# A new kernel of small units: attention by head pairs, the first V turned on TensorE, and a range test of the softmax sums on GpSimd

## The chip, the cores and the metric

The kernel runs on one core of a Trainium2 chip. The metric is the device time of one execution in microseconds (us). TensorE multiplies (PE in the profile, its weight loads PEld), VectorE (DVE) and ScalarE (ACT) evict PSUM and do the pointwise work, GpSimd (POOL) issues the input loads and a few pointwise steps, SyncE (SP) issues the other transfers.

## The reference, cut to what matters

B, H, S, D are 4, 8, 768, 64; a sequence has 8 blocks of 96.

```python
P = sort_net                                   # [B, H, 8, 8]
for _ in range(5):                             # Sinkhorn
    P = exp(P - max(P, -1))
    P = P / (sum(P, -1) + 1e-9)
    P = P / (sum(P, -2) + 1e-9)
k_sorted = einsum('bhij,bhjcd->bhicd', P, k_blocks)   # blocks of K and V mixed by P
v_sorted = einsum('bhij,bhjcd->bhicd', P, v_blocks)
attn = softmax(q_blocks @ k_sorted.T / 8)             # inside each block of 96
x = (attn @ v_sorted) as [B, S, 512]
wq, wk = x @ w_q, x @ w_k                             # 64 wide
mixed = ((wq @ wk.T) / 8) @ x
out = relu(mixed) @ w_out                             # [4, 768, 512] float32
```

Both kernels compute `mixed` as `wq @ (wk.T @ x)`, and neither subtracts the row maximum before the softmax's exponential.

## The kernel before, in words

The kernel has one block of straight code. Work is cut into units, each a small function `u_<letter>(b, n, ...)` with b the batch and n the part, and a string `ORDER` names every unit in the order in which it is recorded. Each engine executes its own instructions in that order and waits on semaphores for the others, so `ORDER` fixes what stands ahead of what on every engine. A capital letter is TensorE work (its last digit is the first PSUM bank), the small letter behind it the eviction of that bank, by ACT (`A`) or DVE (`D`).

The units of one batch, in the order of the data:

- `l`: the loads of Q, K, V on GpSimd's queue, 768 KB each (three buffers of each); `N`: a one-element copy on GpSimd that makes it wait for a certain tile, so that the next load is not issued earlier.
- `c` (lines 150 to 163): the five Sinkhorn rounds, DVE with ACT's exponential, once for all batches. `U`, `b`, `B`: the small matrix is turned on TensorE, copied, and spread over the 128 partitions by eight matmuls with the pattern `Lx`. `n`: M, the block mixing matrix of four heads in the form that TensorE takes, by DVE for batch 0 and by GpSimd for the others, which read `PTR`, an SBUF copy made by `u`.
- `Q`/`q`: Q turned by identity matmuls, a third of the rows of all heads in one unit; `K`/`k`: K sorted and turned in one step, one pair of heads in one unit, out of two banks; `V`/`v`: V sorted, a third of the rows of all heads, evicted to `Vs`.
- `R`: six transfers on SP's queue, 130 KB each, that move the sorted V of a batch from `Vs` into `VT`, where the 96 rows of a block lie on the partitions. All six must have landed before the first `P` of the batch.
- `S`/`e`: scores and exponential for five (block, head pair) items in one unit, seven units a batch; `P`: attention times V, 14 heads' blocks in one unit, five a batch; `r`, `x`: the reciprocals of the sums (column 64 of each product) and the scaled product, DVE.
- `T`/`t`, `J`/`j`, `W`/`w`, `G`/`g`, `H`/`h`, `O`/`o`: the token MLP: X turned, wq and wk, wk turned, wk.T @ x, mixed with relu, output. `d`: half of `qkT` moved by SP to other partitions. `y`: output transfers on SP, a third of a batch each, 512 KB.
- `Z`: matmuls on a zeroed tile `fil` whose result nobody reads, 64 in all; eight at the start, the others between the units of batches 0 and 1.

In S and P of the kernel before an item's number runs over blocks first and head pairs inside a block, so the first group of products needs all four head pairs of K and Q.

Of the kernel before, what the change touches and what calls it, by code (L numbers as in the profile page):

```python
# [14 lines left out]

ORDER = """
l00P l01P l02P i00P i03P i02P l11P c00D Z087 c01D i01D c02D Z027 c03D Z127 c04D Q026 Q007 q02D c05D
Q015 Z224 q01A q00D U006 Z423 b00D Z322 B003 n00D u00A Z522 n11P n01D Z622 K010 K032 n10P k01A K024  # L20
k03D Z727 k02A N02k l03P Z1026 V000 V022 v00A K004 v02D V016 k00A N00k l12P l10P Z821 R01S n21P v01D
R00S K112 S000 R04S S044 n20P e00A k11D S066 e06A R02S K100 e04A S012 R05S S036 R03S k10A Z1125 Z924
e03A K120 K134 e01A k12D S026 e02A k13D P002 S050 r00D Z1227 e05A x00D N00x l21P P014 V106 r01D P030
x01D v10A P042 r04D P024 r03D x04D T007 x03D V112 t00A R10S v11A r02D Q106 x02D R11S Q127 T031 q12A
Q110 q10D T015 t03D q11A N11q l20P l31P l04P l32P l30P T024 V122 t01A S100 n31P v12D S156 t02A J005
e10A n30P S122 R12S j00D J014 R15S e15A K200 R14S j01D W005 R13S e12A w00D W014 S116 w01D G005 e11A
K232 G015 k23A K216 g01D k20A k21D S144 P112 e14A P100 r11D K226 x11D P134 k22A r10D Q213 r13D x10D
S166 Q202 q21A x13D T101 q20A Q220 t10D S134 e16A q22D e13A K322 P146 k32D S250 S214 e25A r14D P122
x14D e21A K330 r12D S246 d00S x12D k33A K304 e24A k30D S220 T123 T112 e22A t12D K314 S236 t11D T133
k31A S260 J102 t13D e23A S204 d01S j10D J113 e26A N26e l22P e20A V306 V310 v30D j11A W102 H024 v31A  # L30
W113 w11D V326 w10D h02D G103 v32A H000 d10S R30S Q312 h00D Q325 q31A G113 q32D Q304 g11A H010 O057
q30D h01A S312 o05D S324 e31A S330 O036 R34S e32A R35S V222 o03D R33S O007 e33A v22D R32S d11S V214
R31S V200 o00D v21A R25S S342 O016 R24S v20D e34A R23S H114 R22S O027 o01D R20S R21S H100 P322 o02A
h11D y00S O046 h10A r32D S304 x32D y01S o04A O107 e30A P240 y02S P232 o10A r24D P214 x24D P226 r23D
r21D O131 x23D O120 r22D o13A x21D T233 o12A P201 x22D t23A S364 y11S O110 e36A r20D T223 x20D o11A
T217 P304 t22A y10S T202 r30D t21A H120 x30D J213 t20A P316 j21D h12A S354 J202 r31D d21S x31D e35A
W213 O141 j20D T300 w21D o14A d20S P334 t30D W207 P342 r33D O156 w20D x33D G207 o15A r34D T311 x34D
T320 y12S t31A G217 t32D T336 g21A J301 t33D H222 H214 j30D J310 h22A d30S W301 H206 j31A w30D O243
h20A d31S W312 G301 o24D h21A O250 w31D O227 o25A G311 y22S o22A O230 g31A H302 H324 o23A O211 h32A
y21S H316 O200 o21D O351 h30D h31A O345 o20A o35D O314 y20S o34D O307 o31A y32S O325 o30A O334 y30S  # L40
o32A o33A y31S
# [4 lines left out]
def kernel(  # L46
# [35 lines left out]
    sb = ctx.enter_context(tc.tile_pool(name="sb", bufs=1))  # L82
# [6 lines left out]
    ENG = {"A": nc.scalar, "D": nc.vector, "P": nc.gpsimd, "S": nc.sync}  # L89
# [8 lines left out]

    def load(t, src, b):
        nc.gpsimd.dma_start(out=t[b % NIN].rearrange("p h r d -> p h (r d)"),  # L100
                            in_=src[b].rearrange("h (p r) d -> p h (r d)", p=P))

    QT = tiles("QT", 2, [P, NP, R6, P])
    KT = tiles("KT", 2, [P, NP, S + P - BLK])
    Vs = tiles("Vs", 2, [P, R6, H, D1])
    VT = tiles("VT", 2, [BLK, NB, H * D1])
    E = tiles("E", 2, [BLK, NT, EW])
    X = tiles("X", 2, [BLK, NB, DM])
    XT = tiles("XT", 2, [P, PT, NB, BLK])
# [4 lines left out]
    mixT = tiles("mixT", 1, [P, 2, 2, R6, P])  # L114
# [3 lines left out]
    R = tiles("R", 4, [BLK, 2, 7], FP32)  # L118
    PTR = sb.tile([P, NB, BH], BF16, name="PTR")
    Pb = sb.tile([BH, NB, NB], BF16, name="Pb")  # L120
    PbT = sb.tile([NB * NB, BH], BF16, name="PbT")
    Lx = sb.tile([NB * NB, NB, NB, SP], BF16, name="Lx")
# [3 lines left out]
    gate = sb.tile([1, 1], BF16, name="gate")  # L126
# [21 lines left out]


    def u_c(b, n, e):  # L150
        if n == 0:
            nc.vector.memset(Pm[:, NB:NB + 1, :], 1e-9)
            nc.vector.memset(fil, 0.0)  # L153
# [3 lines left out]
        nc.scalar.activation(Pv, Pv, ACT.Exp)  # L157
# [3 lines left out]
        nc.vector.reduce_sum(tmp, Pm.rearrange("p i j -> p j i"), axis=AX.X)  # L161
        nc.vector.reciprocal(tmp, tmp)
        nc.vector.tensor_mul(Pb if n == 5 else Pv, Pv, cols(tmp))


    def u_i(b, n, e):
        if n == 0:
            nc.gpsimd.memset(idb, 0.0)
            nc.gpsimd.affine_select(out=idb, in_=idb, compare_op=ALU.not_equal, fill=1.0, base=0,
                                    pattern=[[-1, P]], channel_multiplier=1)  # L170
        elif n == 1:
            nc.vector.reduce_max(m_p, idb.rearrange("p (j s) -> p s j", s=SP), axis=AX.X)
        elif n == 3:
            nc.gpsimd.memset(Lx, 0.0)
            nc.gpsimd.affine_select(out=Lx.rearrange("p i j s -> p (i j) s"),
                                    in_=Lx.rearrange("p i j s -> p (i j) s"),
                                    compare_op=ALU.not_equal, fill=1.0, base=0,
                                    pattern=[[-1, NB * NB], [0, SP]], channel_multiplier=1)
        elif n == 2:
            for t in Vs:  # L180
                nc.gpsimd.memset(t[:, :, :, D:D1], 1.0)
            for t in KT:
                nc.gpsimd.memset(t[:, :, S:S + P - BLK], 0.0)
            for t in E:
                nc.gpsimd.memset(t[:, :, 2 * TH * BLK:EW], 0.0)
                nc.gpsimd.memset(t[:, NT - 1, 2 * (NB * NP - TH * (NT - 1)) * BLK:EW], 0.0)


    def u_l(b, n, e):
        if n == 3:  # L190
            for s, w in enumerate((moe_w_q, moe_w_k)):
                nc.gpsimd.dma_start(out=wqk[:, :, s, :], in_=w.rearrange("(t p) d -> p t d", p=P))
        elif n == 4:
            nc.gpsimd.dma_start(out=wo, in_=moe_w_out.rearrange("(t p) d -> p t d", p=P))
        else:
            load((Qn, Kn, Vn)[n], (q, k, v)[n], b)


    def u_U(b, n, bank):
        mm(bf(bank)[0:NB * NB, 0:BH], Pb.rearrange("p i j -> p (i j)"), idb[0:BH, 0:BH], t=True)  # L200

    def u_b(b, n, e):
        nc.vector.tensor_copy(PbT, bf(U["t"])[0:NB * NB, 0:BH])

    def u_B(b, n, bank):
        for i in range(NB):
            mm(PS[:, bank, i * BH:(i + 1) * BH], Lx[:, i].rearrange("p j s -> p (j s)"), PbT)

    U = {}

    def u_n(b, n, e):
        h0, h1 = n * 4, n * 4 + 4
        if b == 0:
            src = PS[:, U["bank"], 0:NB * BH].rearrange("p (i h) -> p h i", h=BH)
        else:
            src = PTR.rearrange("p i h -> p h i")
        src = src[:, b * H + h0:b * H + h1, :]
        ENG[e].tensor_tensor(  # L218
            out=M[b % 2][:, h0:h1], in0=src.unsqueeze(2).to_broadcast([P, 4, SP, NB]),
            in1=m_p.unsqueeze(1).unsqueeze(3).to_broadcast([P, 4, SP, NB]), op=ALU.mult)  # L220

    def u_u(b, n, e):
        copy(e, PTR.rearrange("p i h -> p (i h)"), PS[:, U["bank"], 0:NB * BH])

# [6 lines left out]
    def u_Q(b, n, bank):  # L231
        ps = bf(bank).rearrange("p (k r s) -> p k r s", k=NP, r=2)
        for r in range(2):
            for kp in range(NP):
                for hh in range(2):
                    mm(ps[hh * D:(hh + 1) * D, kp, r, :], Qn[b % NIN][:, 2 * kp + hh, 2 * n + r, :],
                       idb, t=True)

    def u_q(b, n, e, bank):
        copy(e, QT[b % 2][:, :, 2 * n:2 * n + 2, :].rearrange("p k r s -> p k (r s)"),  # L240
             bf(bank).rearrange("p (k s) -> p k s", k=NP))


    def flat(bank, nb=2):
        return PS[:, bank:bank + nb, :].rearrange("p a n -> p (a n)")

    def u_K(b, n, bank):
        ps = flat(bank)
        for r in range(R6):
            for hh in range(2):  # L250
                h = 2 * n + hh
                mm(ps[hh * D:(hh + 1) * D, r * P:(r + 1) * P], Kn[b % NIN][:, h, r, :],
                   M[b % 2][:, h].rearrange("p s i -> p (s i)"))

    def u_k(b, n, e, bank):
        copy(e, KT[b % 2][:, n, 0:S].rearrange("p (i s r) -> p i s r", i=NB, s=SP),
             flat(bank)[:, 0:S].rearrange("p (r s i) -> p i s r", r=R6, s=SP))


# [6 lines left out]
    def u_v(b, n, e, bank):  # L266
        copy(e, Vs[b % 2][:, 2 * n:2 * n + 2, :, 0:D].rearrange("p r h d -> p h r d"),
             flat(bank).rearrange("p (h r d) -> p h r d", h=H, r=2))

    def u_R(b, n, e):  # L270
        ENG[e].dma_start(out=VT[b % 2].rearrange("(s r) i x -> r s i x", r=R6)[n],
# [198 lines left out]
```

## Time and profile before

| what | us |
|---|---|
| three runs | 125.07, 125.53, 125.67 |
| median | 125.53 |
| span of the profiled execution, first to last instruction | 123.3 |
| busy in it: PE, DVE, ACT, POOL | 101.9, 69.5, 69.2, 27.1 |
| first sorting matmul of K starts / last output matmul ends | 15.0 / 118.6 |

The page gives the profiled execution by its span; the median of the runs is 2.2 us above that span. Line 138 is the helper of all matmuls, lines 142 and 144 those of the copies by ACT and by DVE, so these groups are told apart by their tiles (`ps<-VT,E` is unit P). A matmul's listed duration is a latency of about 0.2 us and more, and successive ones overlap: what a unit costs TensorE is read from the length of a run of many against one of few. PEclk is the granted TensorE clock.

### The profile page before, as it was taken

The numbers are of one execution on the slowest core, as the hardware profiler recorded it, in microseconds if no ns is written. First come the engines' busy times: TensorE is split into PE (matmuls) and PEld (weight loads), VectorE is DVE, ScalarE is ACT, GpSimd is POOL, SyncE is SP. The second block draws the span as 40 slices with busy tenths as digits, with TensorE's granted clock in tenths as the row PEclk, the third lists the DMA queues.
The fourth block names the chain that finished last, engine by engine and source line by source line (L and its number), as shares of the span: only waits on it lengthen the run. The fifth ranks groups of instructions, "written<-read, shape, count | busy, mean of one in ns | idle before, by whom it ended". The sixth has DMA issues, their size and how long they took to land. (4 is left out here: it accounts for less than half of the span.)

```text
span 123.3 us, 3389 instructions
## 1 busy us (share of the span) xinstructions
PE 101.9 (83%) x1439; PEld 65.7 (53%) x1449; DVE 69.5 (56%) x132; ACT 69.2 (56%) x93; POOL 27.1 (22%) x42
## 2 busy tenths in 40 slices
PE   5818877692799999608998999999999999999940
PEld 2216464541447886508887677554767665443410
DVE  2879547305402976404769669497697885304500
ACT  4113155863301699900579977885669736855550
POOL 6993096910020029900000030000000000000000
PEclk9976999999679999995589999999999999999995
DMA  0999999899949426999999339947947104144493
GB/s 4 141 203 203 205 203 153 142 215 227 147 34 203 106 57 57 196 243 206 206 203 206 54 33 175 260 104 202 396 156 308 53 16 175 32 169 171 167 363 153
DMA packets 19950, 20.19 MB, mean 164 GB/s; under 512 B 2016, under 2 KB 18400, under 8 KB 19936
## 3 DMA queue, kind: packets, MB, share of 16 engines
q0 software_dynamic: 14064, 10.09, 56.9%
q1 hardware_dynamic: 5872, 9.89, 24.2%
q8 instruction: 11, 0.18, 0.6%
q14 instruction: 3, 0.02, 0.1%
HBM read 20.19 MB, written 6.29 MB: 215 GB/s over the span
## 5 line engine op out<-in xcount | busy, mean ns | idle before, releaser
L301 ACT ACTIVATE E<-ps 96x960 bf16<-96x960 f32 (+1 forms) x28 | 24.2, 906 | 7.7 <-PE ps L138 7.6
L138 PE MATMUL ps<-wo,mixT 128*128 128x512 bf16 x90 | 22.6, 380 | 0.6 <-issue 0.2
L333 DVE TENSOR_TENSOR X<-ps,R 96x896 bf16<-96x896 f32 (+1 forms) x20 | 19.7, 998 | 0.5
L138 PE MATMUL ps<-fil 128*128 128x512 bf16 x60 | 17.6, 438 | 2.0 <-DVE fil L153 1.2
L138 PE MATMUL ps<-VT,E 96*128 96x65 bf16 x256 | 11.7, 202 | 7.7 <-DMA VT<-Vs 7.2
L138 PEld LDWEIGHTS <-E 96*128 96x128 bf16 x256 | 10.3, 103 | 9.4 <-issue 8.5
L142 ACT COPY ot<-ps 128x512 f32<-128x512 f32 x16 | 9.4, 585 | 10.1 <-PE ps L138 9.2
L138 PEld LDWEIGHTS <-mixT 128*128 128x128 bf16 x96 | 8.2, 98 | 9.4 <-issue 1.3
L328 DVE RECIPROCAL R<-ps 96x14 f32<-96x14 f32 (+1 forms) x20 | 4.3, 222 | 15.4 <-PE ps L138 15.4
L138 PEld LDWEIGHTS <-fil 128*128 128x128 bf16 x64 | 6.5, 110 | 10.0 <-issue 4.4
L138 PE MATMUL ps<-idb,Qn 128*64 128x128 bf16 x192 | 9.2, 263 | 3.1 <-DMA Qn<-in_q_dram 3.1
L142 ACT CAST KT<-ps 128x768 bf16<-128x768 f32 x9 | 7.1, 800 | 6.8 <-PE ps L138 6.8
L142 ACT CAST Vs<-ps 128x1024 bf16<-128x1024 f32 x6 | 6.2, 1029 | 8.1 <-PE ps L138 7.8
L144 DVE CAST KT<-ps 128x768 bf16<-128x768 f32 x7 | 6.6, 956 | 6.7 <-PE ps L138 6.5
L138 PE MATMUL ps<-M,Kn 128*64 128x128 bf16 x192 | 8.3, 227 | 2.2 <-DMA Kn<-in_k_dram 0.9
L138 PEld LDWEIGHTS <-Qn 128*64 128x64 bf16 x192 | 7.7, 138 | 4.3 <-DMA Qn<-in_q_dram 3.6
L138 PE MATMUL ps<-QT,KT 64*128 64x96 bf16 x256 | 9.8, 207 | 0.2 <-ACT KT L142 0.2
L144 DVE COPY ot<-ps 128x512 f32<-128x512 f32 x8 | 5.5, 689 | 7.6 <-ACT ot L142 4.8
L406 ACT ACTIVATE mixT<-ps 128x1024 bf16<-128x1024 f32 x8 | 8.1, 1029 | 2.7 <-PE ps L138 2.6
L144 DVE CAST Vs<-ps 128x1024 bf16<-128x1024 f32 x6 | 7.2, 1222 | 3.0 <-PE ps L138 3.0
L138 PEld LDWEIGHTS <-Kn 128*64 128x64 bf16 x192 | 6.4, 113 | 4.5 <-issue 2.5
L218 POOL TENSOR_TENSOR M<-PTR,m_p 128x512 bf16<-128x512 bf16 x6 | 7.7, 1321 | 5.0 <-ACT PTR L142 4.9
(67 smaller groups left out, 132.9 us busy)
## 6 DMA issues: line engine op xcount, KB each, us to landing
out_dram<-ot SPq DMA_DIRECT2D x12, 512.0 KB, 2.8
VT<-Vs SPq DMA_DIRECT2D x24, 130.0 KB, 4.6
Qn<-in_q_dram POOLq DMA_DIRECT2D x4, 768.0 KB, 11.0
Kn<-in_k_dram POOLq DMA_DIRECT2D x4, 768.0 KB, 10.9
Vn<-in_v_dram POOLq DMA_DIRECT2D x4, 768.0 KB, 11.5
wo<-in_moe_w_out_dram POOLq DMA_DIRECT2D x1, 512.0 KB, 14.7
qD<-qkT SPq DMA_DIRECT2D x8, 48.0 KB, 2.3
wqk<-in_moe_w_q_dram POOLq DMA_DIRECT2D x1, 64.0 KB, 3.5
```

The source lines that it names most:

```text
L138: nc.tensor.matmul(o, w, x, is_transpose=t, start=start, stop=stop, skip_group_check=True)
L142: nc.scalar.copy(o, i)
L144: nc.vector.tensor_copy(o, i)
L218: ENG[e].tensor_tensor(out=M[b % 2][:, h0:h1], in0=src.unsqueeze(2).to_broadcast([P, 4, SP, NB]), in1=m_p.unsqueeze(1).unsqueeze(3).to_bro ...
L301: nc.scalar.activation(E[b % 2][:, n, 0:2 * w * BLK].rearrange("p (t a c) -> p a t c", a=2, c=BLK), PS[0:BLK, bank:bank + 2, 0:w * BLK].re ...
L328: nc.vector.reciprocal(rr[b, n][:, :, 0:w], avps(bank, w)[:, :, :, D])
L333: nc.vector.tensor_mul(xo.rearrange("p (a t d) -> p a t d", a=2, d=D), avps(bank, w)[:, :, :, 0:D], rr[b, n][:, :, 0:w].unsqueeze(3).to_br ...
L406: nc.scalar.activation(o, i, ACT.Relu)
```

## The change

- **Order.** `ORDER` is a new list with another order, other banks and other engines for the evictions. The `N` units are gone. Batch 0's loads are cut in halves (K's first half first); the loads of batch 1 follow without a wait.
- **Units by head pairs.** Q becomes four units of one head pair (768 columns) in place of three of 1024; S, P and X run over head pairs first and blocks inside, so the first scores need only the first pair. T turns one head pair (eight blocks) in one unit, and X, XT are laid out for that. H is three equal units of 256 columns, `mixT` has two buffers. W turns 128 rows in place of 64.
- **First V on TensorE.** For batch 0, V and its six transfers R are replaced by Y/y (sorted and turned as K is, into the other K tile) and F/f (turned back by 32 identity matmuls, and evicted straight into `VT`). Batches 1 to 3 keep V, v and R, with one `Vs` buffer in place of two.
- **Start.** `PbT` is made by DVE's transpose in place of U and b; `Lx` is made by an ACT copy from the identity and `m_p` by eight small matmuls and an ACT copy, in place of GpSimd's and DVE's steps; M of batch 0 is made by head pairs. The first `Z` unit has 28 matmuls and stands behind the matmuls for `m_p`; one other `Z` unit of two is left.
- **Range test and general path.** All reciprocals are kept in one tile `Rall` (96 partitions x 280). After everything that GpSimd does, `guard()` reduces it to its maximum and, negated in place, to its minimum, loads a flag into a register, and `tc.If` runs `general()` if a value lies outside 1e-20 to 1e20. `general()` computes the whole reference again with GpSimd alone. Its 14,528 instructions (with the waits among them) stand between GpSimd's part and the end; the other engines have none of it. With the inputs here it is jumped over.
- **End.** Batch 3's outputs leave in six transfers of 256 KB, the others as before.

```diff
 ORDER = """
-l00P l01P l02P i00P i03P i02P l11P c00D Z087 c01D i01D c02D Z027 c03D Z127 c04D Q026 Q007 q02D c05D
-...
+i02:D lk0a i00:G lq0a c00:D lq0b a01:A c01:D a02:A lk0b c02:D lv0a Z028:0 Q02:0 a03:A Q00:1 c03:D
+a04:A lv0b Q03:2 c04:D a05:A lp i03:G c05:D B00:3 n03:D:3 q03:A:2 Q01:4 n00:D:3 n02:D:3 q00:A:1 lq1
+K03:5 q01:D:4 lk1 u00:A:3 K02:1 k03:A:5 K00:4 n01:D:3 k02:D:1 q02:A:0 Y00:6 lv1 Y01:0 y00:D:6 K01:2
+Y03:6 k00:A:4 y01:A:0 S00:4 y03:A:6 n11:G F00:0 F03:1 f03:D:1 k01:A:2 Y02:6 n10:G y02:D:6 S05:2
+F01:1 e00:A:4 S01:4 F02:6 n21:G e05:A:2 e01:A:4 f02:D:6 S02:2 Q11:7 Q12:4 e02:A:2 f00:A:0 Q10:6
+...
+h11:A:6 O15:5 r32:D:0 P33:6 P31:2 W21:4 o15:A:5 O13:5 w21:A:4 r31:D:2 s02:S
+r33:D:6 O12:4 x33:D:6 x32:D:0 o13:A:5 s10:S P30:6 O14:5 W20:0 T32:1 x31:D:2 w20:A:0 d20:S T31:2
+t32:A:1 G20:3 r30:D:6 d21:S x30:D:6 G21:3 T30:6 g20:A:3 o14:D:5 t31:D:2 T33:7 H22:0 t30:D:6 o12:A:4
+...
+    def u_a(b, n, e, bank):
+        nc.scalar.activation(Pv, Pv, ACT.Exp)
+        if n == 2:
+            for j in range(NB):
+                mm(PS[:, 7, 0:SP], idb, idb[:, j * SP:(j + 1) * SP], start=(j == 0), stop=(j == NB - 1))
+            nc.scalar.copy(m_p, PS[:, 7, 0:SP])
+        elif n == 3:
+            nc.scalar.copy(Lx.rearrange("p a j s -> p (a j) s"),
+                           idb[0:BH, 0:BH].unsqueeze(2).to_broadcast([BH, BH, SP]))
...
+        if n == 5:
+            nc.vector.transpose(PbT, Pb.rearrange("p i j -> p (i j)"))
...
+    def u_Y(b, n, bank):
+        sort_turn(Vn, b, n, bank)
+    def u_y(b, n, e, bank):
+        in_blocks(KT[(b + 1) % 2], n, e, bank)
+    def u_F(b, n, bank):
+        for i in range(NB):
+            mm(bf(bank)[0:BLK, i * P:(i + 1) * P], KT[(b + 1) % 2][:, n, i * BLK:(i + 1) * BLK], idb, t=True)
+    def u_f(b, n, e, bank):
+        copy(e, VT[b % 2][:, :, 2 * n:2 * n + 2, 0:D],
+             bf(bank)[0:BLK, :].rearrange("p (i h d) -> p i h d", i=NB, h=2))
...
-            i, kp = divmod(pr, NP)
+            kp, i = divmod(pr, NB)
...
-        nc.vector.reciprocal(rr[b, n][:, :, 0:w], avps(bank, w)[:, :, :, D])
+        nc.vector.reciprocal(Rall[:, b, n, :, 0:w], avps(bank, w)[:, :, :, D])
...
+    def guard():
+        s1 = keep.tile([1, 2], FP32, name="s1")
+        flag = keep.tile([1, 1], mybir.dt.int32, name="flag")
+        g = nc.gpsimd
+        rv = Rall.rearrange("p b n a t -> p (b n a t)")
+        g.tensor_reduce(s1[:, 1:2], rv, axis=AX.XYZWC, op=ALU.max)
+        g.tensor_scalar(rv, rv, -1.0, None, op0=ALU.mult)
+        g.tensor_reduce(s1[:, 0:1], rv, axis=AX.XYZWC, op=ALU.max)
+        g.tensor_scalar(s1[:, 0:1], s1[:, 0:1], -1e-20, None, op0=ALU.is_le)
+        g.tensor_scalar(s1[:, 1:2], s1[:, 1:2], 1e20, None, op0=ALU.is_le)
+        g.tensor_tensor(s1[:, 0:1], s1[:, 0:1], s1[:, 1:2], op=ALU.mult)
+        g.tensor_scalar(flag, s1[:, 0:1], -1.0, 1.0, op0=ALU.mult, op1=ALU.add)
+        return g.value_load(flag[0:1, 0:1])
...
+    off = guard()
+    work.close()
+    with tc.If(off > 0):
+        with tc.tile_pool(name="gp", bufs=1) as gp, \
+                tc.tile_pool(name="gd", bufs=1, space=bass.MemoryType.DRAM) as dram:
+            general(nc.gpsimd, gp, dram)
```

More of the change, by code (lines that the diff above doesn't have):

```diff
@@ L24 @@
[L24 to L28, printed above, removed]
@@ new lines @@
+t12:D:4 e20:A:6 Q30:4 t13:D:3 S25:0 q32:D:5 H00:2 S26:6 q30:D:4 Q31:5 J10:4 e25:A:0 h00:D:2 e26:A:6
+lk3 S23:0 H02:6 S24:2 R21:S h02:D:6 j10:A:4 q31:D:5 O00:4 e23:A:0 K30:0 e24:A:2 R25:S k30:A:0 Q33:7
+R23:S R20:S o00:D:4 K32:2 k32:D:2 H01:5 P23:0 r23:D:0 x23:D:0 lv3 J11:4 h01:A:5 j11:A:4 P22:2 P20:5
+r22:D:2 x22:D:2 r20:D:5 O04:4 V30:0 P24:2 x20:D:5 d11:S r24:D:2 q33:A:7 o04:A:4 O01:7 v30:A:0
+o01:A:7 W11:4 K31:5 x24:D:2 K33:0 s00:S V31:2 w11:A:4 k33:D:0 T22:4 k31:A:5 d10:S T23:5 V32:6
+v31:A:2 P21:0 t23:A:5 W10:2 v32:A:6 t22:D:4 r21:D:0 O02:3 S32:4 R31:S w10:D:2 S36:6 G10:2 G11:2
@@ L170, in u_i @@
                                     pattern=[[-1, P]], channel_multiplier=1)
-        elif n == 1:
-            nc.vector.reduce_max(m_p, idb.rearrange("p (j s) -> p s j", s=SP), axis=AX.X)
-        elif n == 3:
[L174 to L183, printed above, removed]
+        elif n == 2:
+            nc.vector.memset(Pm[:, NB:NB + 1, :], 1e-9)
+            nc.vector.memset(fil, 0.0)
+            for t in KT:
+                nc.vector.memset(t[:, :, S:S + PAD], 0.0)
+        elif n == 3:
@@ L191, in u_l @@
+            nc.gpsimd.memset(Rall[:, :, NG - 1, :, (NU - AG * (NG - 1)) // 2:AG // 2], 1.0)
+    def u_l(b, n, e, bank):
+        if n == "p":
             for s, w in enumerate((moe_w_q, moe_w_k)):
                 nc.gpsimd.dma_start(out=wqk[:, :, s, :], in_=w.rearrange("(t p) d -> p t d", p=P))
-        elif n == 4:
+        elif n == "o":
             nc.gpsimd.dma_start(out=wo, in_=moe_w_out.rearrange("(t p) d -> p t d", p=P))
         else:
-            load((Qn, Kn, Vn)[n], (q, k, v)[n], b)
@@ L199, in u_U @@
[L199 to L203, printed above, removed]
+            t, src = {"q": (Qn, q), "k": (Kn, k), "v": (Vn, v)}[n[0]]
+            h0, h1 = {"": (0, H), "a": (0, H // 2), "b": (H // 2, H)}[n[2:]]
+            b = int(n[1])
+            nc.gpsimd.dma_start(out=t[b % NIN][:, h0:h1].rearrange("p h r d -> p h (r d)"),
+                                in_=src[b, h0:h1].rearrange("h (p r) d -> p h (r d)", p=P))
@@ L205, in u_B, with u_u @@
     def u_B(b, n, bank):
         for i in range(NB):
[L207 to L212, printed above, removed]
+            g, x = divmod(i, BH // NB)
+            mm(PS[:, bank, i * BH:(i + 1) * BH], Lx[:, x].rearrange("p j s -> p (j s)"),
+               PbT[:, g * BH:(g + 1) * BH])
+    def u_u(b, n, e, bank):
+        copy(e, PTR.rearrange("p i h -> p (i h)"), PS[:, bank, 0:NB * BH])
@@ L213, in u_n @@
+    def u_n(b, n, e, bank):
         if b == 0:
-            src = PS[:, U["bank"], 0:NB * BH].rearrange("p (i h) -> p h i", h=BH)
+            h0, hn = 2 * n, 2
+            src = PS[:, bank, 0:NB * BH].rearrange("p (i h) -> p h i", h=BH)
         else:
+            h0, hn = 4 * n, 4
             src = PTR.rearrange("p i h -> p h i")
-        src = src[:, b * H + h0:b * H + h1, :]
+        src = src[:, b * H + h0:b * H + h0 + hn, :]
         ENG[e].tensor_tensor(
-            out=M[b % 2][:, h0:h1], in0=src.unsqueeze(2).to_broadcast([P, 4, SP, NB]),
-            in1=m_p.unsqueeze(1).unsqueeze(3).to_broadcast([P, 4, SP, NB]), op=ALU.mult)
@@ L222, in u_u @@
-    def u_u(b, n, e):
-        copy(e, PTR.rearrange("p i h -> p (i h)"), PS[:, U["bank"], 0:NB * BH])
+            out=M[b % 2][:, h0:h0 + hn], in0=src.unsqueeze(2).to_broadcast([P, hn, SP, NB]),
+            in1=m_p.unsqueeze(1).unsqueeze(3).to_broadcast([P, hn, SP, NB]), op=ALU.mult)
     def u_Z(b, n, bank):
@@ L231, in u_Q, with sort_turn @@
     def u_Q(b, n, bank):
[L232 to L237, printed above, removed]
-    def u_q(b, n, e, bank):
[L240 to L247, printed above, removed]
+        for r in range(R6):
+            for hh in range(2):
+                mm(bf(bank)[hh * D:(hh + 1) * D, r * P:(r + 1) * P],
+                   Qn[b % NIN][:, 2 * n + hh, r, :], idb, t=True)
+    def u_q(b, n, e, bank):
+        copy(e, QT[b % 2][:, n].rearrange("p r s -> p (r s)"), bf(bank)[:, 0:S])
+    def sort_turn(src, b, n, bank):
         ps = flat(bank)
@@ new lines @@
+        if kind == "l":
+            u_l(0, item[1:].split(":")[0], None, None)
+            continue
+        name = item.split(":")[0]
+        b, n = int(name[1]), int(name[2:])
+        if kind.isupper() and kind != "R":
+            fns[kind](b, n, int(arg[0]))
+        else:
+            fns[kind](b, n, arg[0], int(arg[1]) if len(arg) > 1 else None)
+    off = guard()
[4 more added lines that the diff above has]
+            general(nc.gpsimd, gp, dram)
```

350 lines of the change are left out of this document (231 added, 119 removed).

## The prediction

> **What bounds the kernel now.** I read the page first, for the two strips of TensorE and its clock.
>
> ```profile
> PE 101.9 (83%) x1439; PEld 65.7 (53%) x1449; DVE 69.5 (56%) x132; ACT 69.2 (56%) x93; POOL 27.1 (22%) x42
> PE   5818877692799999608998999999999999999940
> PEclk9976999999679999995589999999999999999995
> ```
>
> TensorE is busy for 83% of the span, but not evenly: from slice 20 on (62 us) it is full, before that it has holes, and behind three of them the clock row falls to 5 to 7. The groups say what part of the 101.9 us is empty work, and the waits what the holes wait for:
>
> ```profile
> L138 PE MATMUL ps<-fil 128*128 128x512 bf16 x60 | 17.6, 438 | 2.0 <-DVE fil L153 1.2
> PE ps L138 <- DMA VT<-Vs: 7.2, 2, 4.5
> VT<-Vs SPq DMA_DIRECT2D x24, 130.0 KB, 4.6
> ```
>
> 17.6 us go to `fil`, and 7.2 us in two waits for the transfers R, which take 4.6 us (median) to land. The timeline and 5 us windows place them:
>
> ```profile
> 31.23 0.61 PE L138 MATMUL ps<-VT,E 96*128 96x65 bf16 x14 [2.72 <-DMA VT<-Vs]
> 33.04 5.60 PE L138 MATMUL ps<-fil 128*128 128x512 bf16 x20 [0.22 <-issue]
> 55.85 1.70 PE L138 MATMUL ps<-VT,E 96*128 96x65 bf16 x28 [4.53 <-DMA VT<-Vs]
> ```
>
> ```profile
> 45.00:50.00 5.00, 4.95 (x97) 3.58 (x96) 2.92 (x5) 4.94 (x7) 4.50 (x7) 1.00 0.60 69
> 50.00:55.00 5.00, 1.28 (x30) 0.92 (x26) 1.36 (x2) 2.40 (x4) 2.52 (x2) 1.00 1.22 223
> 55.00:60.00 5.00, 4.15 (x70) 3.79 (x70) 2.17 (x5) 0.80 (x1) 0.00 (x0) 0.58 1.29 209
> 100.00:105.00 5.00, 5.00 (x61) 2.83 (x60) 3.20 (x6) 2.72 (x5) 0.00 (x0) 1.00 0.27 108
> ```
>
> The window's columns are PE, PEld, DVE, ACT, POOL busy, clock, DMA share, GB/s. In 50 to 55 no engine works while the loads fill the DMA engines (223 GB/s), and the clock behind it is 0.58. So the first 72 us are bound by transfers and the order, the rest by TensorE.
>
> **Method.** I price every unit from the rows, sum each engine's units over a stretch of the order, and take the larger sum, times what such stretches needed before. TensorE, from runs at full clock (many against few of one kind): S 21 ns a matmul (10 in 0.39, 30 in 0.81), K 27.5, Q 30, P 32 (14 in 0.61, 50 in 1.77), T 42, V 56, G 54, J 163, O 217; an H unit 0.22 us. ACT and DVE by the groups: exponential 0.975 us (ACT), K copy 0.80/0.956 (ACT/DVE), V copy 1.03/1.22, relu 1.03/1.22, output copy 0.585/0.69, X 1.08 and R 0.23 (DVE). New shapes: the Q copy of 768 columns as the XT copy of that size (0.81/0.555); Y as K, its copy as K's; F's 128-wide turns as V's matmuls; F's copy lies between XT's 768 columns (0.81/0.555) and QT's 1024 (1.01/0.68), and I take the latter, its size; the wk copy on ACT between 0.28 (DVE) and 0.47 (ACT's qkT), 0.30 taken.
>
> These prices against before: from the first G of batch 1 (73.9) to the last O (118.6), 44.7 us for 40.1 us of TensorE units, 1.115 times. ACT-bound: from P of batch 0, part 3 (38.5) to the hole at 51.3, 12.8 us for 12.0, 1.07; from 55.85 to 71.4, 15.5 for 13.2, 1.18 (with the half clock). I take 1.10.
>
> **Part by part.** Totals hardly move. TensorE loses one V (1.34 us) and gains four Y (1.32) and four F (1.79): 70.7 us of units against 68.9, without `fil`. ACT goes from 71.4 to 72.4, DVE from 64.7 to 66.0. So the change buys no work; it can only remove the holes, of which before has 118.6 - 15.0 - 68.9 = 35 us between the first K and the last O.
>
> *Start.* The Sinkhorn chain ends at 12.6 (Pb, 12.41 + 0.21). Behind it U, b and B took until 14.1; now a DVE transpose (between the 0.15 of the PbT copy and the 0.38 of the m_p reduction; 0.25) and B (0.36). M by pairs needs half of 0.69 before the first K. K starts at about 13.9, in place of 15.0. The 28 `fil` wait for the identity (about 3), run as before's first twelve (4.40) plus 16 x 0.21, and end near 11, ahead of B: nothing. The steps taken off GpSimd free its queue 2.4 us earlier (950 + 1499 ns), and nobody waited for that.
>
> *13.9 to the first P.* ACT 12.5, DVE 7.0, TensorE 7.2. ACT bounds. No R stands in it: the 2.7 us wait and the 20 `fil` (5.6 us, until batch 0's next P) go. What is late next is ACT, and behind it the load of V: input moves at 203 GB/s from about 4 us (before: 768 KB of Q used at 8.7), 3.9 us a load; so K and V of batch 1 land near 25 and 29, the first V of batch 1 is due near 31. Covered by 2 us; if that cover is gone, V's delay comes on top one to one.
>
> *P of batch 0 to P of batch 1:* DVE 4.3, then ACT 11.1. *To the first H:* DVE 8.9. *To P of batch 2:* DVE 5.2. Sum of the four stretches 12.5 + 4.3 + 11.1 + 8.9 + 5.2 = 42.0, times 1.10 = 46.2. Without `N`, loads of batch 2 stand in the queues when batch 1's R go out. Six R are 0.78 MB, 3.8 us at 203 GB/s alone, and 8.3 us is the longest landing before; between the last V copy and the first P of batch 1 stand some 4 us of TensorE units. I take 1 us of wait (between 0 and 4.3). P of batch 2 starts at 13.9 + 46.2 + 1 = 61.
>
> *Rest.* TensorE 39.0, ACT 30.4, DVE 30.4: TensorE bounds, 39.0 x 1.115 = 43.5, to 104.6. Then a copy, a transfer and the end: 4.7 us before (118.6 to 123.3), 4.3 with half the bytes. Span 108.9, and 2.2 as before around it: 111.1. With small dependences inside the new units open, I say 111.5.
>
> *Range test.* It starts behind the last R-reciprocal; after that TensorE still has 15.4 us of units (17 with the factor), and the end 4.3. Cover: 21 us, less DVE's lag on the last P, 16 at least.
>
> ```profile
> L175 POOL TENSOR_SCALAR_AFFINE_SELECT Lx<-Lx 64x1024 bf16<-64x1024 bf16 x1 | 1.5, 1499 | 0.1
> L287 POOL COPY gate<-KT 1x1 bf16<-1x1 bf16 x2 | 0.4, 176 | 0.7 <-ACT KT L142 0.7
> ```
>
> GpSimd's rows give 1.46 ns (this one) to 2.58 ns an element (M, 1321 ns for 512): three passes over 280 elements are 1.2 to 2.2 us, four tiny steps 0.7. The reductions across partitions, the register load and the jump over the general path show in no row; for the jump, the smallest transfer's 1.7 us. Some 5 us, hidden. As for the reductions, the nearest row is a pass by partition, which I take; the other bound is the second rival.
>
> **Rivals.** *The order does not hold (0.14).* A transfer or a bank keeps engines idle as R did: against it speaks that batch 0 has no R; for it, that the loads run unchecked. One hole as at 55.85 in each of batches 1 and 2, 4.5 us less the 1 us counted, with some 3 us of slow matmuls behind: 117 to 122.
>
> *The reductions are slow (0.08): slower than before.* If GpSimd goes through the 96 partitions one after another, each takes 96 x 280 x 1.46 ns = 39 us, both 78; with 3 us around and 16 to 21 of cover, the end moves by 60 to 65 us, to about 174. It decides above roughly 7 us a reduction; 13 us each would already lose the gain. The Trainium skill (GPSIMD Engine Reference, Cross-partition — where GPSIMD wins) gives 247.7 us for a reduction along partitions of 128x2048; 280 columns by that would be an estimated 34 us each, and the result about 164. No row here shows it; what speaks against it is that all columns are folded too, so that one crossing of partitions is enough.
>
> *The clock falls without `fil` (0.10).* Before, idle TensorE of 2.7 us (31.2) and 4.5 us (55.85) was followed by matmuls at half speed for 4 to 6 us; gaps of 0.9 us were not. In 13.9 to 60 TensorE has 31 us of work in 46 us, with nothing to fill it. At half speed throughout it would need 62 x 1.1 = 68 us, 22 more: 133. The slack is 46 - 31 x 1.1 = 12 us, so 12 us of its work at half speed would be hidden, and with 25 us of it the gain is used up. The holes that I can place (waits for ACT's copies) are 1 to 1.5 us: slow in places, 115 to 124 (0.04); through most of the stretch, up to 133 (0.06). The Trainium skill (TensorE: Matmul & The Clock Gate, What's actually happening) names an idle window of about 3.4 us as the cause; our 2.7 us was enough, so the measurement decides, and by the page's figure this case would be rarer still.
>
> *The holes go, but nothing comes of it (0.02):* 125.
>
> **Numbers.** Forecast 0.66, 105 to 117. The range 105 to 122 adds the order rival: 0.80. About 0.5% is what a measurement of this kernel tells from no change. Faster: 0.66 + 0.14 + 0.04 = 0.84; same 0.02; slower: 0.08 + 0.06 = 0.14.
>
> **What would show it.** Right: no `VT<-Vs` wait of batch 0; K at 14, first P at 26 to 28, P of batch 2 near 61, last O near 105; ACT at 4.5 of 5 us in 15 to 42; guard steps done by 100. Wrong: PEclk below 9 between 14 and 60 (clock); PE waiting for VT, Kn or Vn over 2 us (order); a POOL row of TENSOR_REDUCE over 7 us, with the chain of what ended last on POOL (reductions).

## The result, and the profile after

The changed kernel takes 110.99 us (median of 4 runs, 109.91 to 111.24) beside 125.34 us for the kernel before on the same chip: a ratio of 0.886, with a 95% interval of 0.879 to 0.893. Forecast were 111.5 us and 105 to 122. The profiled execution took 111.22 us, of which 107.8 are the span. Here and below a median takes all executions, and a ratio with its interval only those within 1.5% of the fastest execution of the same kernel.

The page of the changed kernel, its busy line and the strips of 40 slices (2.7 us each):

```profile
PE 93.6 (87%) x1485; PEld 64.8 (60%) x1494; DVE 69.8 (65%) x139; ACT 70.1 (65%) x102; POOL 27.7 (26%) x45
PE   0999978997878894389999999999999999999950
PEclk9999999999999999955799999999999999999998
DMA  0899999999999999999999600447067108009793
```

One dent is left in TensorE's row (slices 15 and 16) and one in its clock, just behind it. From slice 18 on TensorE is full. The DMA row is full up to slice 21, 59 us: by then nearly all input has been moved. The groups, waits and transfers that answer to the lines shown of before:

```profile
L146 PE MATMUL ps<-fil 128*128 128x512 bf16 x29 | 9.1, 481 | 0.3 <-ACT Vs L150 0.3
PE ps L146 <- DMA VT<-Vs: 1.8, 1, 1.8
PE ps L146 <- DMA Kn<-in_k_dram: 2.3, 2, 1.7
VT<-Vs SPq DMA_DIRECT2D x18, 132.0 KB, 4.2
```

`fil` fell from 17.6 to 9.1 us, nearly all of it ahead of the first K; the waits for VT from 7.2 to 1.8 us; the transfers R from 24 to 18. The timeline of TensorE in the changed kernel gives the dates of the prediction's steps (start, duration, idle time before in brackets):

```profile
13.79 0.53 PE L146 MATMUL ps<-M,Kn 128*64 128x128 bf16 x12
25.43 0.81 PE L146 MATMUL ps<-VT,E 96*128 96x65 bf16 x20
43.45 0.86 PE L146 MATMUL ps<-M,Kn 128*64 128x128 bf16 x24 [1.69 <-DMA Kn<-in_k_dram]
46.09 0.93 PE L146 MATMUL ps<-VT,E 96*128 96x65 bf16 x14 [1.78 <-DMA VT<-Vs]
62.57 0.61 PE L146 MATMUL ps<-VT,E 96*128 96x65 bf16 x14
```

These are the first K, the first P of batch 0, K of batch 2, and the first P of batches 1 and 2. The windows around the dent (PE, PEld, DVE, ACT, POOL busy, clock, DMA share, GB/s):

```profile
40.00:45.00 5.00, 2.62 (x66) 2.05 (x64) 2.73 (x5) 2.64 (x5) 1.55 (x2) 1.00 1.24 240
45.00:50.00 5.00, 3.90 (x66) 3.61 (x66) 1.86 (x4) 1.65 (x3) 0.00 (x0) 0.58 1.31 206
50.00:55.00 5.00, 5.00 (x87) 4.25 (x86) 3.85 (x7) 3.29 (x5) 0.00 (x0) 0.74 1.31 205
```

Two waits within 4 us, and behind them 6.4 us at half clock: P with 14 products takes 0.93 us for 0.61.

The chain of what ended last shows where the second wait comes from (three of its pieces; start, duration):

```profile
11.78 19.47 DMA Vn<-in_v_dram
38.80 7.16 DMA VT<-Vs
46.09 14.44 PE ps L146 x273
```

The load of batch 1's V landed at 31.25, its copies and the transfers R followed, and the last R ended at 45.96, just ahead of the first P of batch 1.

**Where the time came from.** I cut the time from 14 us to TensorE's last product into windows of 1 us and summed three things: busy time times the granted clock (work, in us at full clock), busy time lost to the clock, and idle time.

| kernel | work | lost to the clock | idle | sum |
|---|---|---|---|---|
| before | 88.1 | 4.9 | 12.0 | 105 |
| changed | 79.3 | 3.3 | 7.4 | 90 |

The difference of 15 us is 8.8 of work (`fil` inside the order, for the most part), 4.6 idle and 1.7 of clock. These are single executions: a second one of the changed kernel (after_again, below) gives 79.2, 4.4 and 6.3. (Records of some products are missing in the traces, so the first column is good to about 1 us.)

### The profile page after: what moved, and what is told of

Read it like the earlier page. It is cut to its first block, busy times and chain, and to the rows that moved or that the text cites. A ratio compares the mean times of both kernels' runs of the same rounds, so it can differ in the third digit from the quotient of the medians.

```text
span 107.8 us, 3487 instructions
## 1 busy us (share of the span) xinstructions
PE 93.6 (87%) x1485; PEld 64.8 (60%) x1494; DVE 69.8 (65%) x139; ACT 70.1 (65%) x102; POOL 27.7 (26%) x45
## 4 chain that ended last, share of the span: by engine, by line
PE 56%; DMA 32%; ACT 2%; POOL 2%; issue 2%; DVE 2%; SPq 1%; POOLq 0%; ACTq 0%
PE ps L146 56%; DMA Vn<-in_v_dram 18%; DMA Qn<-in_q_dram 7%; DMA VT<-Vs 7%; ACT Vs L150 2%; DVE Vs L152 1%; POOL Kn L218 1%; POOL Qn L218 1%; ACT ot L150 1%; DVE XT L152 1%; SPq L301 1%; POOL idb L190 0%; POOL idb L189 0%; POOLq L190 0%; ACTq L150 0%
## 5 line engine op out<-in xcount | busy, mean ns | idle before, releaser
L345 DVE TENSOR_TENSOR X<-ps,Rall 96x896 bf16<-96x896 f32 (+1 forms) x20 | 19.9, 1005 | 0.6
L150 ACT CAST KT<-ps 128x768 bf16<-128x768 f32 x13 | 10.1, 803 | 6.5 <-PE ps L146 6.4
L437 POOL CROSS_LANE_REDUCE s<-Rall 96x1 f32<-96x280 f32 x1 | 0.8, 757 | 45.3 <-DVE Rall L340 45.3
L239 POOL TENSOR_TENSOR M<-PTR,m_p 128x512 bf16<-128x512 bf16 x6 | 7.9, 1317 | 15.0 <-PE ps L146 12.7
L146 PEld LDWEIGHTS <-KT 64*128 64x128 bf16 (+1 forms) x288 | 8.8, 98 | 4.1 <-issue 2.2
L146 PE MATMUL ps<-QT,KT 64*128 64x96 bf16 x256 | 10.1, 207 | 0.5 <-ACT E L316 0.3
L150 ACT CAST Vs<-ps 128x1024 bf16<-128x1024 f32 x8 | 8.1, 1015 | 2.4 <-PE ps L146 2.3
L146 PE MATMUL ps<-fil 128*128 128x512 bf16 x29 | 9.1, 481 | 0.3 <-ACT Vs L150 0.3
L152 DVE COPY XT<-ps 128x768 bf16<-128x768 bf16 x13 | 6.7, 552 | 3.8 <-PE ps L146 3.8
L340 DVE RECIPROCAL Rall<-ps 96x14 f32<-96x14 f32 (+1 forms) x20 | 4.4, 225 | 6.4 <-PE ps L146 5.4
L407 DVE TENSOR_SCALAR mixT<-ps 128x1024 bf16<-128x1024 f32 x6 | 7.3, 1224 | 1.6 <-PE ps L146 1.1
L405 ACT ACTIVATE mixT<-ps 128x1024 bf16<-128x1024 f32 x6 | 5.9, 1021 | 2.5 <-PE ps L146 2.5
```

What stands on the lines that cost most here:

```text
L146: nc.tensor.matmul(o, w, x, is_transpose=t, start=start, stop=stop, skip_group_check=True)
L150: nc.scalar.copy(o, i)
L152: nc.vector.tensor_copy(o, i)
L239: ENG[e].tensor_tensor(out=M[b % 2][:, h0:h0 + hn], in0=src.unsqueeze(2).to_broadcast([P, hn, SP, NB]), in1=m_p.unsqueeze(1).unsqueeze(3). ...
L340: nc.vector.reciprocal(Rall[:, b, n, :, 0:w], avps(bank, w)[:, :, :, D])
L345: nc.vector.tensor_mul(xo.rearrange("p (a t d) -> p a t d", a=2, d=D), avps(bank, w)[:, :, :, 0:D], Rall[:, b, n, :, 0:w].unsqueeze(3).to_ ...
```

## The experiments

They ran in three groups, each beside runs of the kernel before on the same chip: median 125.14 us in the first (11 runs), 124.62 in the second (16), 125.0 in the third (11). The ratios are to these runs of before, taken as said above, with 95% intervals.

### First group: the test, and the dent at 42 to 46 us

**The changed kernel again** (after_again) is the yardstick.

> The changed kernel itself, so that the others of this group are compared on one chip: 110.5 to 111.3 us, span 107.5 to 108.6, by every theory.

Measured: 110.27 us, ratio 0.887 (0.878 to 0.895).

**No range test** (no_test): the guard and the general path are left out.

```diff
-    off = guard()
-    work.close()
-    with tc.If(off > 0):
-        ...
-            general(nc.gpsimd, gp, dram)
```

> Left out: the range test and the general path (guard and general), nothing else. If the test lies wholly under the last output stage (its seven steps end at 90.9 of 107.8 us), the time stays within 0.5 us of the changed kernel. Rival: the long GpSimd program costs at the start or the end (the changed kernel's time lies 3.4 us above its span, before's 2.2): then it is about 1 us faster, with the same span.

Measured: 110.36 us, ratio 0.886 (0.878 to 0.893). The test costs nothing that can be measured. Its rows in the changed kernel's timeline of GpSimd:

```profile
86.83 0.76 POOL L437 CROSS_LANE_REDUCE s<-Rall 96x1 f32<-96x280 f32 x1 [45.28 <-DVE Rall L340]
88.05 0.93 POOL L438 TENSOR_SCALAR Rall<-Rall 96x280 f32<-96x280 f32 x1 [0.47 <-DVE X L345]
89.06 0.76 POOL L439 CROSS_LANE_REDUCE s<-Rall 96x1 f32<-96x280 f32 x1
90.74 0.18 POOL L443 TENSOR_SCALAR flag<-s 1x1 int32<-1x1 f32 x1
```

**`wo` loaded late** (wo_late): that load, 512 KB, stood ahead of the loads of batch 2.

```diff
-... x01:D:4 r03:D:6 lo x03:D:6 ... R10:S lv2 K23:4 ...
+... x01:D:4 r03:D:6 x03:D:6 ... R10:S lv2 lo K23:4 ...
```

> One edit: the load of w_out (512 KB) is issued behind the load of batch 2's V, not ahead of batch 2's loads. If the hole of TensorE at 41.7 to 46.1 us comes from the filled DMA queues, K of batch 2 lands some 2.5 us earlier (512 KB at 203 GB/s): its wait of 1.7 us goes, the wait for VT (1.8) shrinks, the clock does not fall to 0.58 behind it, and the time drops by 3 to 5 us, to 106 to 108. Rival: the transfers of VT are bound by SP's own issue (0.55 to 1.4 us each) or by the V copies, then the hole only moves: at most 1.5 us faster. Second rival: TensorE was not what set the end there (ACT and DVE behind it), under 1 us.

Measured: 111.44 us, ratio 0.888 (0.876 to 0.899). No gain. The wait for K of batch 2 is gone, but both first P now wait for VT (its timeline):

```profile
45.14 0.59 PE L142 MATMUL ps<-VT,E 96*128 96x65 bf16 x14 [3.58 <-DMA VT<-Vs]
62.50 0.59 PE L142 MATMUL ps<-VT,E 96*128 96x65 bf16 x14 [2.08 <-DMA VT<-Vs]
```

P of batch 2 starts at 62.50, as in the changed kernel, though TensorE was ready 2.1 us sooner.

**The dent filled** (fill_hole): two runs of 8 products of `fil`.

```diff
-... w01:A:3 Q20:1 K20:6 ... R12:S P10:2 ...
+... w01:A:3 Q20:1 Z18:2 K20:6 ... R12:S Z18:0 P10:2 ...
```

> Two edits: eight matmuls on the zeroed tile ahead of the unit K of batch 2, part 0, and eight ahead of the first P of batch 1, where TensorE waits 1.7 and 1.8 us. If the half clock of 46 to 53 us costs what its units lost (P 0.93 for 0.61, two K 1.49 for 0.86, two P 1.72 for 1.06, and so on, 2.6 us in all) and TensorE sets the end there, the time drops by 1.5 to 2.6 us with the hole still in place. Rival: the slow units were hidden behind ACT or DVE, or the added matmuls delay as much as they win: within 0.7 us of the changed kernel.

Measured: 111.32 us, ratio 0.890 (0.881 to 0.899). The clock stayed full through the dent (1.00 from 40 to 60 us), and P of batch 2 still began at 62.05, after a wait of 2.80 us for VT. Its first P and a window behind it:

```profile
62.05 1.04 PE L143 MATMUL ps<-VT,E 96*128 96x65 bf16 x14 [2.80 <-DMA VT<-Vs]
65.00:70.00 5.00, 5.00 (x51) 3.37 (x50) 3.46 (x6) 2.46 (x4) 0.00 (x0) 0.64 0.04 10
```

In this execution (112.51 us, mean granted clock 0.965) the half clock was moved behind the new wait: by the account 3.3 us are lost to the clock, as in the changed kernel, but all of them after 62 us. Two other executions had a mean clock of 0.992, so almost no half clock, and took 110.17 and 110.23 us; after_again took 109.53 to 111.13 at 0.953 to 0.984. So curing the half clock is worth nothing that shows either, and the reason read from the trace is that VT lands at 62.

wo_late and fill_hole together gave a new theory: up to P of batch 2 the transfers set the date. All input (10.1 MB) and two batches of R (1.58 MB) at 203 GB/s, from 4 us on, end at 61.5 us.

### Second group: less traffic, and the parts of the change one by one

**V of batch 3 not loaded** (no_v3_load): `lv3` is dropped from `ORDER`, and V of batch 3 is computed from V of batch 0.

> Left out: the load of batch 3's V (its V is computed from what lies in the buffer, batch 0's). Nothing waits for this load before 66 us, so it matters only by the queue that it fills. Traffic theory: 0.79 MB less, R of batch 2 lands up to 3.9 us earlier, P of batch 2 starts at 59 to 60 (62.6 now), the time drops by 2 to 3.5 us, to 107 to 108.5. Rival, ACT and the order as the bound, or R limited by SP's issue: within 0.8 us of the changed kernel.

Measured: 111.38 us, ratio 0.902 (0.894 to 0.911). The traffic theory's gain did not come. Two rows of the changed order without that load, a window and the first P of batch 2:

```profile
55.00:60.00 5.00, 5.00 (x120) 4.02 (x119) 4.75 (x9) 4.69 (x7) 0.00 (x0) 1.00 0.30 74
63.03 0.61 PE L142 MATMUL ps<-VT,E 96*128 96x65 bf16 x14
```

The DMA engines are nearly empty from 55 us (74 GB/s for 230 in the changed kernel), P of batch 2 waits for nothing, and it starts at 63.03 all the same: now TensorE comes late, because the dent and the half clock behind it (clock 0.56 in 50 to 55) are unchanged. So there seem to be two limits of about the same date: the landing of VT near 62, and TensorE after dent and half clock, near 62 to 63. Each run so far lifted one of them.

**V of batch 1 turned on TensorE too** (v1_turned): the six R of batch 1 go.

```diff
-V12:0 ... v12:A:0 ... V10:6 ... V11:6 ... R14:S R15:S ... R11:S ... R10:S ... R13:S ... R12:S
+Y12:0 ... y12:A:0 ... F12:4 ... f12:D:4 ... (four Y and four F, as batch 0 has them; no R)
```

> V of batch 1 also turned on TensorE (four Y, four F in place of three V and six R; first P of batch 1 ahead of K of batch 2). Traffic theory: 0.79 MB less, as above, and no wait for VT in batch 1: P of batch 1 starts near 43 (46.1 now), P of batch 2 at 59 to 60, the time is 107 to 109. Rival, ACT as the bound: TensorE has 1.8 us more, ACT and DVE 3.6 us more between 31 and 43, P of batch 1 starts no earlier, the time is 111 to 113.

Measured: 110.12 us, ratio 0.883 (0.872 to 0.894): the same as the changed kernel. TensorE waits for VT nowhere up to P of batch 2, at 62.43. In the account of the table: work 83.0, clock 1.7, idle 5.4, together 90 again. Turning costs TensorE 3.7 us of work and takes away 3.6 us of idle time and half clock: an exchange without profit. Its first P of batch 1 starts at 45.95 (46.09 changed) although no R stands ahead of it, so there, too, TensorE's date lies close to that of the transfers. The time lies between the two expected ranges.

**V of batch 0 by transfers again** (v0_by_transfer): the changed order with before's V, v and R for batch 0.

```diff
-Y00:6 ... y00:D:6 ... F00:0 ... f00:A:0 ...   (four Y, four F)
+V00:6 ... v00:D:6 ... R00:S R01:S ...         (three V, six R)
```

> One part undone: V of batch 0 again by V, v and six transfers R in the places of Y and F, the rest of the new order kept. Traffic theory: until 62 us the filled DMA queues are the bound, all loads (10.1 MB) and the R of two batches (1.6 MB) pass at 203 GB/s from 4 us on, 4 + 57.5 = 61.5, and the first P of batch 2 starts then, whatever TensorE does before. Six more R are 0.79 MB, 3.9 us: P of batch 0 starts at 29 to 31 (25.4 now), P of batch 2 near 66, the time is 113.5 to 115. Rival, ACT as the bound up to 60 us: ACT and DVE lose 3.6 us of copies, the wait for R is caught up: within 1.5 us of the changed kernel.

Measured: 116.92 us, ratio 0.937 (0.923 to 0.951). In its timeline P of batch 0 comes at 30.77, after 2.77 us of waiting for VT, in place of 25.43, as expected. P of batch 1 then waits 3.92 us, and P of batch 2 starts at 70.58 in place of the expected 66, so the part is worth more than expected. In the account (14 to 112 us): work 75.0, clock 10.9, idle 12.1. Against the changed kernel that is 4.3 us less work, but 4.7 more idle and 7.7 more lost to the clock, a term that the expectation left out. (The profiled execution took 117.54 us, the four 114.92 to 117.74, so these differences are on the large side; but the mean clock was low in all four, 0.88 to 0.91.)

**Before without its fillers** (before_no_fill): the kernel before, with thirteen groups of products of `fil` taken out of its order (`Z027`, `Z127` and so on).

> The kernel before without its later matmuls on the zeroed tile (56 of 64; the eight at the start stay). If they only stood in holes that the transfers make, the time stays at 124 to 126.5 (clock a little lower behind the holes). Rival, they kept the clock up where it counted: 127 to 130. Rival, they delayed the work behind them: 121 to 123, and that much of the gain would be theirs.

Measured: 121.4 us, ratio 0.983 (0.977 to 0.989): faster than before, although its waits grew, as its list of waits shows:

```profile
PE ps L142 <- DMA VT<-Vs: 10.5, 2, 5.9
```

In the account: work 79.1, clock 5.7, idle 16.2, together 101 in place of 105. The fillers bought 0.8 us of clock and filled 4.2 us of idle time at a price of 9.0 us of TensorE; queued ahead of real work, they were in its way for the difference. The second group of P of batch 0 shows it, with the fillers (timeline of before) and without:

```profile
38.48 0.62 PE L138 MATMUL ps<-VT,E 96*128 96x65 bf16 x14
32.98 0.95 PE L142 MATMUL ps<-VT,E 96*128 96x65 bf16 x14
```

It is at half clock without them, and still 5.5 us earlier. These two profiled executions differ by 4.4 us; by the ratio the fillers cost 2.1 us, so the account overstates them.

Read as a chain, the ratios part the gain of 0.113: the fillers 0.017 (2.1 us), the order and the smaller units, with the start, the end and the test, 0.046 (5.7 us), V of batch 0 on TensorE 0.050 (6.3 us). By the intervals above, the last two are good to about 0.016 each, an estimate, so which of them is larger is not shown; the parts were measured in this sequence only, and the order was not separated from the units.

### Third group: both limits, the tail, the cover of the test

**K and V of batch 3 into the buffers of batch 2** (kv3_buf), with `wo` late; **the same with 8 products of `fil`** ahead of the first P of batch 1 (kv3_buf_fill).

```diff
-            nc.gpsimd.dma_start(out=t[b % NIN][:, h0:h1]...
+            nc.gpsimd.dma_start(out=t[2 if b == 3 and n[0] in "kv" else b % NIN][:, h0:h1]...
```

> The changed kernel with wo loaded late (as before in this study) and K and V of batch 3 loaded into the buffers of batch 2 instead of batch 0, so that those two loads (768 KB each) start only when TensorE is done with K and V of batch 2, near 47 and 54 us, and not at 40. Everything is still computed. Theory of two limits: up to P of batch 2, TensorE (its wait at 42 to 46 us and the half clock behind it) and the transfers (VT of batch 2 lands near 62 us) come out at the same time, so that lifting one alone (wo late, the hole filled, V of batch 3 not loaded) gave nothing; with both lifted P of batch 2 starts at 58.5 to 60.5 us and the rest, 41.5 us of TensorE, follows: 107 to 109 us. Rival: the last transfers of VT are set by SP's issues and their own latency and not by the loads beside them: P of batch 2 stays near 62, 110 to 111.5 us.

> As the other kernel with K and V of batch 3 in the buffers of batch 2 and wo late, and 8 products of fil (about 2 us) on TensorE ahead of the first P of batch 1, where TensorE waits for VT. Theory of two limits: the clock stays full after the wait, which saves up to 1.7 us more where the wait would have been, P of batch 2 at 58 to 60 us: 106 to 108.5 us. Rival: as the hole filled alone, P of batch 2 waits for VT until 62: 110.5 to 112 us.

Measured: 114.89 us (112.28 to 115.67; no interval for the ratio) and 114.40 us, ratio 0.912 (0.903 to 0.920). Both are slower than the changed kernel (by 3.1 us in the second, by the ratios), above the theory and above the rival of each. In kv3_buf's trace P of batch 2 starts at 66.14. The second kernel's chain of what ended last, and its P of batch 2:

```profile
55.43 6.51 DMA VT<-Vs
62.07 0.93 PE L143 MATMUL ps<-VT,E 96*128 96x65 bf16 x14 [3.10 <-DMA VT<-Vs]
```

TensorE got to R of batch 2 sooner (first issue 49.92, in the changed kernel 53.47), yet the last of them took 6.51 us, while V of batch 3, now issued at 52.48, was on its way at the same time (206 and 198 GB/s in 50 to 60). The load was moved from ahead of R onto R. P of batch 2 waited 3.10 us, and half clock came behind it (0.93 us for 14 products): the dent of batch 1 had been traded for one of batch 2. This run therefore does not decide what lifting both limits would bring; a run with `wo` late and V of batch 3 left out would have, and it was not made. That stays open.

**Half of O in batches 1 and 2** (half_o).

```diff
-        for t in range(PT):
+        pt = 2 if b in (1, 2) else PT
+        for t in range(pt):
```

> The changed kernel, in which O of batches 1 and 2 sums two of its four products of 128 rows (the other two are left out: 24 products 128x512 fewer, at 0.22 to 0.25 us each from one to the next, 5.2 to 6 us, nearly all behind 74 us). Theory that TensorE alone sets the time from 62 us on: the whole of it comes off, 104.5 to 106 us. Rival: the copies out of ps on ACT and DVE, whose number is unchanged, or the stores set the pace as soon as TensorE is a little faster: 108 to 110.5 us.

Measured: 107.9 us, ratio 0.865 (0.857 to 0.873). By the ratios about 2.7 us of the 5.2 or more came off: between the two theories. Part of the rest went to VT: in the profiled execution P of batch 2 waited 2.20 us for it, as in wo_late, and 1.7 us were lost to the clock behind that; this execution took 109.01 us, the three others 107.0 to 108.57, so they may have lost less. And in its chain of what ended last, DVE and ACT stand between TensorE's pieces, where the changed kernel's chain has TensorE alone from 46.09 us to 104.01:

```profile
84.17 3.09 DVE X L345 x3
87.31 4.48 PE ps L146 x60
91.81 0.57 DVE qkT L152
92.40 1.27 PE ps L146 x12
```

So TensorE sets the time from 62 us on in the changed kernel, but the copies of DVE and ACT follow so closely that they come forward as soon as it has less to do. How the missing 2.5 us or more divide between the copies and the wait was not separated.

**A longer test** (long_test).

```diff
+        for _ in range(24):
+            g.tensor_reduce(s1[:, 1:2], rv, axis=AX.XYZWC, op=ALU.max)
```

> The changed kernel with 24 more reductions over all of Rall in the range test, at the 0.76 us of the profile: 18.2 us. Theory (the test lies on GpSimd alone and ends at 90.9 us, 17 us ahead of the span's end, and only the branch behind it is waited for): it ends at 109.1 us, the span becomes 109 to 111, the time 111.5 to 114 us, some 1.5 to 3 above the changed kernel. Rival: the test is not hidden or takes turns with VectorE: 18 us or more on top, 126 to 130 us. Other rival: more reductions of the same data overlap (0.4 us each as the nearest rows had it): it ends near 101 us and nothing is added, 110 to 111.

Measured: 119.53 us, ratio 0.958 (0.949 to 0.966): more than the first theory (111.5 to 114) and far less than its rival. The test in the timeline of GpSimd, and the span:

```profile
87.98 19.88 POOL L439 CROSS_LANE_REDUCE s<-Rall 96x1 f32<-96x280 f32 x24
110.64 0.18 POOL L445 TENSOR_SCALAR flag<-s 1x1 int32<-1x1 f32 x1
core 0: 117.5 us, clock 0.919
```

The reductions took 0.83 us each from start to start, one after another, and the test ended at 110.82. But the span ends 6.7 us after that. No engine has a row in that stretch; the DMA view of it shows two packets of the instruction queue (0.02 MB) and nothing else. So what follows the test takes 6.7 us when it comes last. In the program the register load and the jump over the general path stand there; the trace does not divide them.

## Why the prediction was right, and where it was not

The steps of the sum, from the timelines above:

| step | predicted | measured |
|---|---|---|
| first K | 13.9 | 13.79 |
| K to the first P (12.5 x 1.10) | 13.75 | 11.6 |
| P of batch 0 to P of batch 1 (15.4 x 1.10, and 1 us of wait) | 17.9 | 20.7 |
| P of batch 1 to P of batch 2 (14.1 x 1.10) | 15.5 | 16.5 |
| P of batch 2 to the last O | 43.5 | 41.4 |
| end of the span | 4.3 | 3.8 |
| around the span | 2.2 | 3.4 (2.2 in after_again) |

The steps are off by -0.1, -2.1, +2.8, +1.0, -2.1, -0.5 and +1.2 us. They nearly cancel, so that the time came out within 0.5 us of the forecast is in part luck.

- **Start: right.** K came 0.1 us from its date.
- **K to the first P: right in kind.** No R in it, ACT nearly full (4.51 and 4.97 us in 15 to 20 and 20 to 25). The factor of 1.10, taken from stretches of before, was too much here: 11.6 us is below the 12.5 us of units, and P came at 25.4, ahead of the 26 to 28 given. ACT was busy for 11.12 us of the stretch. Its successive rows overlap by some 0.1 us (a copy of QT is listed from 15.45 to 16.27, the next row starts at 16.14), so a sum of group means counts too much.
- **The wait of 1 us for VT: mis-sized, and it was one of two.** I had looked for one wait. K of batch 2 waits first (1.69 us; gone in wo_late, so `wo` stood in its way), then VT (1.78). I had not checked K of batch 2 at all. V of batch 1, the other load that I did check, landed at 31.25 in place of 29, and TensorE waited for it (0.59 us, and 0.57 for K of batch 1): the cover of 2 us was gone, and the chain of this execution runs from that load over R to the first P of batch 1. No engine was full in this stretch: of its 20.7 us TensorE worked 15.1, ACT 14.8 (where the sum had it as the bound, with DVE) and DVE 12.7. ACT at 4.5 of 5 us, named as a sign, held up to 25 us only (4.06 and 3.58 in the next two windows).
- **The clock rival: its condition came true in one place.** The prediction put slow matmuls outside its forecast; the account has 3.3 us lost to the clock, and PEclk shows the sign given, 5, 5 and 7 in slices 17 to 19. The order rival's sign was met as well (2.3 us of waits for Kn), without its price. The half clock cost little in the changed kernel: the executions of fill_hole nearly without it were no faster. But v0_by_transfer lost 10.9 us to the clock, so part of what turning V of batch 0 gains is clock, and the prediction had not counted that.
- **P of batch 2 at 61: nearly the right number, but not for the reason given.** I had DVE bound that stretch. From 46.09 to 62.57 DVE worked 12.5 of 16.5 us and ACT 12.0, but TensorE 16.4, at a mean clock of 0.80. wo_late, fill_hole and no_v3_load point to two limits: the landing of VT, and TensorE after its dent, both near 62 us. A run with both lifted is missing.
- **The rest: right in kind.** TensorE is busy throughout (idle 0.35 us from 62 to 104); in half_o about half of what was taken off TensorE came off the time, so it is the bound, with others close behind. The factor was 41.4 / 39.0 = 1.06 in place of 1.115.
- **The range test: hidden, as forecast, but longer than priced.** The reductions took 0.76 us, so the rival of slow ones is out. The 34 us that the Trainium skill's figure gave for each (GPSIMD Engine Reference, Cross-partition — where GPSIMD wins) is far from this row. The cover was right: from the test's first row at 86.83 to the end of the span it is 21 us. The mis-sized term is the jump, priced at 1.7 us by the smallest transfer; with the register load it stands for 6.7. So the test takes 4.1 + 6.7 = 10.8 us in place of some 5, and 10.2 us of cover are left. long_test gives the same number: the test ended 19.9 us later (110.82 for 90.92) and the span 9.7 us later (117.5 for 107.8).
- **That the holes, with the fillers in them, hold the gain: right.** before_no_fill and v0_by_transfer show the parts, with the clock as a term beside them; TensorE's work beside the fillers stayed what it was, as the sum had it (79.1 us in before_no_fill, 79.3 changed).
- **One reading of before was loose.** In 50 to 55 us engines still worked (TensorE 1.28 us, GpSimd 2.52); the hole itself lies from 51.3 to 55.85.

No version of this study that computes the whole result beats the changed kernel by more than the measurement can tell; v1_turned, 110.12 us, is level with it.

## What to carry to other kernels

A wait that looks worth 3 us in the profile may be worth nothing, because another limit has the same date: lift it in one run, look where the next start stays, and only then decide what the bound is. Filler products in an in-order queue cost their whole length where the wait ends early, so compare the kernel without them before tuning them. A step that is hidden is hidden only up to a point, and making the step longer shows what follows it unseen, which two dates in the first trace do not.

## What the runs showed of the hardware

- **The clock fell after less idle time than before showed.** In v1_turned, TensorE idled for 1.29 us (37.1 to 38.4), with another 0.32 us shortly before, and ran at half clock from 38.9 to 42.3. Its windows, with the clock third from the end:

```profile
37.00:38.00 1.00, 0.11 (x6) 0.00 (x0) 1.00 (x2) 1.00 (x2) 0.00 (x0) 1.00 1.32 206
39.00:40.00 1.00, 1.00 (x6) 0.55 (x5) 0.00 (x0) 1.00 (x2) 0.00 (x0) 0.50 1.32 204
42.00:43.00 1.00, 0.94 (x19) 0.63 (x14) 0.00 (x0) 1.00 (x2) 1.00 (x1) 0.85 1.14 192
```

  The Trainium skill (TensorE: Matmul & The Clock Gate, What's actually happening) puts the fall after an idle window of about 3.4 us; the trace has it after 1.29. The length of one wait does not decide it: in no_v3_load 1.65 us of idle time ahead of 19.00 us left the clock at 1.00. What does decide it was not tested.
- **A reduction over all 96 partitions and 280 columns takes GpSimd 0.76 us**, less than its pass over the same data by partition (0.93).
- **The end behind a conditional block**: 6.7 us from the last step of the test to the end of the span in long_test, with nothing in it but two instruction packets.
- **Small transfers behind large loads**: an R of 132 KB landed 2.3 us after its issue at best and 7.2 us at worst in the changed kernel, the longest, of batch 1, while loads and transfers together moved 225 to 240 GB/s (5 us windows from 35 to 45 us).
